# Which score VectorE copies, where v's sums go, and the order of a phase's last four scores

## The chip, the cores and the metric

One core of a Trainium2 chip runs the whole program. The metric is the device time of one execution in microseconds (us). The core has a matrix engine (TensorE: PE in the profile, its weight loads PEld), VectorE (DVE), ScalarE (ACT), GpSimd (POOL) and SyncE (SP), which here issues transfers. Each engine takes its instructions in the order in which they were written, and waits on semaphores for the others. PSUM, the memory that TensorE writes, has eight banks; a tile of 128 x 512 float32 fills one of them.

## What is computed

The kernel mixes a full attention and a token-mixing MLP over the same x (2048 tokens, 512 channels, 32 heads of 16).

```python
g = _sigmoid((x * gate_w).sum(-1, keepdims=True))
# A: attention
q, k, v = split_heads(x @ wqkv)
p = _softmax(einsum("bhqd,bhkd->bhqk", q, k) * Dh ** -0.5)
a = merge_heads(einsum("bhqk,bhkd->bhqd", p, v)) @ wo
# B: token mixing
h = _layernorm(x)
u = _gelu(einsum("bsd,sf->bdf", h, w1) + b1)
b = einsum("bdf,fs->bds", u, w2) + b2, transposed
out = g * a + (1 - g) * b
```

## The kernel before

The first 278 us project v, k and q, and compute the first layer of the MLP. From there to 1232 us runs one long loop, and the change lies in it. The loop has 32 groups (a pair of heads and half of the queries) of 4 phases each, 128 phases in all, numbered p from 0.

**A phase.** A phase computes 16 blocks of scores, numbered n from 0 to 15; a block has 128 keys by 512 queries of one head and fills one PSUM bank. Each block's exp is then multiplied with v, and the products are added up in a PSUM tile `av`. The two heads of a pair lie in the two halves of TensorE's rows, so a score needs only half of the rows. The other half works beside it on a matmul of other work, called dense here (L1049): the MLP's second layer, late parts of the q projection, or the output projection. A phase has either 14 dense matmuls (96 phases, "14-phases") or 12 (32 phases, "12-phases": two in a row at p = 6, 14, 22 and so on to 62, and the last 16, p = 112 to 127). Scores that have no dense partner are written for the other head than the one before them, so that two can run side by side.

**Who evacuates the scores.** ScalarE takes six blocks one by one (`SINGLE`, L1066: exp straight from PSUM) and four as two pairs (`TWO`, L1004: exp over two banks). VectorE copies the other six to SBUF (`EVAC`, L1062), four early in the phase and n = 14 and 15 at its end; one exp over all six (L1075, 128 x 3072) follows. An empty instruction of VectorE (`mark`, L1084) stands behind the copies and gathers waits for that exp. The pairs in `TURNS` are multiplied with v in the same phase, those in `HELD` (the copied ones) in the next.

**Banks.** Seven banks serve the scores, the eighth (`dn`) the dense work. `share` lists the seven for a phase. Scores 0 to 6 take `share[0]` to `share[6]`, scores 7, 8 and 9 take `share[0]`, `[1]`, `[2]` once more, and 10 to 15 take `[3]`, `[4]`, `[5]`, `[6]`, `[0]`, `[1]`. What is left, `share[2]`, becomes `av`. A matmul into a bank waits until the score before it in that bank is read.

**Sums.** At the end of a phase VectorE adds `av` to the group's sums in SBUF (L961). In a group's first phase there are two tiles: `av` closes the group before (from the held pairs), and a second one, in the place of a score pair (`t`), begins the new group. How many adds a tile takes depends on which heads and query halves its pairs hold: all four together are one add of 128 x 512, three of the four are one of 128 x 256 and one of 64 x 256.

**Order around it.** Engines run the loop in the order of the source. `calls` are transfers issued at a phase's beginning, `amid` is work of VectorE that is written ahead of its copy of score 14, and `later` is work of VectorE that is written after the phase's copies, ahead of the adds. The last two blocks of the MLP's gelu (functions `inner`, `tanh`, `outer`, L555 to L565) are spread over `later` of phases 0 to 3. `add_manual_dep(one..., earlier...)` makes the third single exp (n = 4) wait for the second pair's exp of the phase before, on ScalarE itself.

Of the kernel before, what the change touches and what calls it, by code (L numbers as in the profile page):

```python
# [60 lines left out]
def gated_mix(ctx: ExitStack, tc: tile.TileContext, a_x, a_wqkv, a_wo, b_w1, b_b1, b_w2, b_b2, gate_w, out):  # L61
    nc = tc.nc
# [487 lines left out]
        late_u.append((u, at))  # L550
    late_s = o_pool.tile([P, ND, NB], F32, name="big0")

    def inner(i):
        u, s = late_u[i][0], late_s[:, i, :]
        nc.vector.tensor_mul(s, u, u)  # L555
        nc.vector.tensor_scalar(s, s, GELU_A, 1.0, ALU.mult, ALU.add)
        nc.vector.tensor_mul(s, s, u)

    def tanh(i):
# [2 lines left out]
    def outer(i):  # L562
        u, at = late_u[i]
        nc.vector.scalar_tensor_tensor(u, late_s[:, i, :], 1.0, u, ALU.add, ALU.mult)
        split(u_hi[:, at, :], u_lo[:, at, :], u, nc.vector.tensor_copy, nc.vector.tensor_tensor)  # L565

    acc_ctx.close()
# [113 lines left out]
    def on_dve(at, *what):  # L681
        later.setdefault(at, []).append(what)
# [54 lines left out]
    def invert(half, k, pairs, at):  # L737


        n = pairs * 2  # L740
        w = QW // DH
        t = out_pool.tile([P, w], F32, name="inv")[: n * DH]
        nc.sync.dma_start(t, r_d[half][k][:n].rearrange("r (a b) -> (r a) b", b=w))

        def turn():
            nc.vector.tensor_scalar_max(t, t, LEAST_SUM)
            nc.vector.reciprocal(t, t)

        def put_back():
            nc.sync.dma_start(ri_d[half][k][:n].rearrange("r (a b) -> (r a) b", b=w), t)  # L750

        if half and k == ND - 1:
            amid[at + 1] = [turn]
# [91 lines left out]
        return put(steps, at, [len(steps)])  # L845

    for i in range(2):
        on_dve(i, inner, i)
        on_dve(1 + i, tanh, i)
        on_dve(2 + i, outer, i)  # L850
    call(3, load_xt, 2)
    for b in range(ND):
        call(6 + b, nc.sync.dma_start, v_d[b], vb[b][:, :BV])
# [39 lines left out]

    token, mark = (out_pool.tile([1, 1], F32, name=name, bufs=1) for name in ("token", "mark"))

    EVAC = 1, 3, 5, 7, 14, 15
    SINGLE = 0, 2, 4, 6, 8, 9
    TWO = (10, 11), (12, 13)
    TURNS = [(0, 2), (4, 6), (8, 9), *TWO]
    HELD = [(1, 3), (5, 7), (14, 15)]  # L900

    def shares(n):

# [62 lines left out]
    with tc.manual_schedule(engines=engines):  # L966
# [3 lines left out]
        for p in range(LAST + 1):  # L970
# [14 lines left out]
            n_b = len(beside)  # L985
            half = slice(0, HALF) if second else slice(HALF, P)

            alone = NSC - (NSC - n_b) // 2
            head = [second if n < alone else 1 - second for n in range(NSC)]
            in_turn = list(range(n_b)) + [n for pair in zip(range(n_b, alone), range(alone, NSC)) for n in pair]  # L990
            qbs = {}
            for a, b in TURNS + HELD:
                if head[a] == head[b]:
# [21 lines left out]
            for n in in_turn:  # L1015
# [3 lines left out]
                if n < TWO[0][0]:  # L1019
                    if n >= BANKS:  # L1020
                        ones[share[n - BANKS]] = psum.tile([P, NB], F32, name=f"s{share[n - BANKS]}")
                    s = ones[share[n % BANKS]]
                else:
                    if n == TWO[0][0]:
                        pool.__exit__(None, None, None)
                        pool = regions()
                        psum = pool.__enter__()
                        twos = {}
                        for low in range(BANKS):
                            if low == share[2]:  # L1030
# [9 lines left out]
                nc.tensor.matmul(  # L1040
                    s,
# [5 lines left out]
                if n < n_b:  # L1047
# [4 lines left out]
                    if n == n_b - 1:  # L1052
                        fence = nc.gpsimd.memset(token, 0.0)  # L1053
                        tc.add_manual_dep(fence.ins, mm.ins.name, SYNC, reason=REASON)
                if n == HELD[-1][0]:
                    if n_b and second and beside[-1][-1] in between:
                        between[beside[-1][-1]]()
                    for what in amid.get(p, ()):
                        what()
                if n in EVAC:  # L1060
                    pt = evac[:, EVAC.index(n), :]
                    nc.vector.tensor_copy(pt, s)  # L1062
# [1 line left out]
                elif n in SINGLE:  # L1064
                    pt = ptp.tile([P, NB], F32, name="p1", bufs=len(SINGLE))
                    one = nc.scalar.activation(pt, s, AF.Exp, scale=SCALE)  # L1066
# [25 lines left out]
                what(*args)  # L1092
# [186 lines left out]
```

## Time and profile before

| | |
|---|---|
| time, median of 3 runs | 1267.92 us (1267.75 to 1268.17) |
| profiled execution | 1267.55 us, of which the span is 1265.7 |
| PE busy in the span | 1257.1 us (99%) |
| ACT busy | 1071.2 us (85%) |
| DVE busy | 849.1 us (67%) |
| POOL busy | 199.3 us (16%) |
| granted TensorE clock, mean | 0.999 |

The profile is of one execution. A row of the timeline reads: start in us from the span's start, length in us, engine, line of the kernel, operation, what it writes and reads by the program's names, how many were merged, and in brackets the idle time of the engine before it with what ended that. Merged rows overlap, since an instruction's length runs from its start to its result and the next one starts earlier. PE counts as busy while a matmul is in flight, modelled, so a full PE row does not say that TensorE could not go faster.

### The profile page before, as it was taken

How to read it: one execution, taken by the hardware profiler on the slowest of the kernel's cores; microseconds unless marked ns; L12 is line 12 of the kernel's file. 1: busy time of each engine (PE TensorE's matmuls, PEld its weight loads, DVE VectorE, ACT ScalarE, POOL GpSimd, SP SyncE). 2: the span in 40 equal slices, each digit the busy share in tenths (PEclk: the TensorE clock that was granted, in tenths of full speed). 3: DMA queues.
4: the chain of work that ended last, by engine and by line, in shares of the span. 5: the costliest groups of instructions: out<-in, count | busy, mean ns of one | idle time of the engine just before them, and what ended most of it. 6: DMA issues, size and time to landing. Idle time of an engine off the chain costs nothing.

```text
span 1265.7 us, 32791 instructions
## 1 busy us (share of the span) xinstructions
PE 1257.1 (99%) x13342; PEld 838.1 (66%) x13342; DVE 849.1 (67%) x1547; ACT 1071.2 (85%) x1405; POOL 199.3 (16%) x316
## 2 busy tenths in 40 slices
PE   9999999999999999999999999999999999999998
PEld 7888888875666666666666666666666666666666
DVE  5675453178767676767677677776777677678883
ACT  4443343269999999999999999999999999999990
POOL 0220444461010101010110101111111111000000
PEclk9999999999999999999999999999999999999999
DMA  4799443243744544544344433444543443366511
GB/s 134 253 327 342 139 125 104 79 130 96 223 123 100 93 101 85 156 87 97 77 103 96 95 92 85 91 87 80 114 100 76 88 99 60 56 166 176 143 65 70
DMA packets 100555, 152.31 MB, mean 120 GB/s; under 512 B 17109, under 2 KB 56171, under 8 KB 96300
## 3 DMA queue, kind: packets, MB, share of 16 engines
q1 hardware_dynamic: 99820, 149.08, 46.0%
q8 instruction: 107, 1.75, 0.6%
q10 hardware_dynamic: 576, 1.05, 0.2%
q14 instruction: 52, 0.43, 0.1%
HBM read 105.39 MB, written 44.68 MB: 119 GB/s over the span
## 4 chain that ended last, share of the span: by engine, by line
PE 98%; DVE 1%; ACT 1%; DMA 0%; issue 0%; SPq 0%
PE av L939 31%; PE s L1040 22%; PE acc L424 12%; PE acc L75 8%; PE t L1040 8%; PE t L939 5%; PE dn L1049 5%; PE u L1040 4%; PE pa L1131 2%; PE acc L199 1%; PE acc L268 1%; DVE pe L1062 0%; PE pa L1161 0%; ACT p L1066 0%; DMA wv_raw<-in_A_wqkv_dram 0%; ACT pe L1075 0%
## 5 line engine op out<-in xcount | busy, mean ns | idle before, releaser
L1066 ACT ACTIVATE p<-s 128x512 f32<-128x512 f32 x768 | 406.2, 726 | 0.4
L1075 ACT ACTIVATE pe<-pe 128x3072 f32<-128x3072 f32 x129 | 375.6, 2913 | 0.4 <-DVE mark L1084 0.4
L1040 PE MATMUL s<-qs,ks 64*128 64x512 f32 x1280 | 330.1, 400 | 0.8 <-DVE ot L961 0.8
L1062 DVE COPY pe<-s 128x512 f32<-128x512 f32 x512 | 318.0, 684 | 4.6 <-PE s L1040 1.1
L1040 PEld LDWEIGHTS s<-qs,ks 64*128 64x128 f32 x1280 | 225.8, 184 | 91.8 <-issue 51.9
L1004 ACT ACTIVATE p<-t 128x1024 f32<-128x1024 f32 x256 | 268.6, 1188 | 0.0
L939 PE MATMUL av<-p,v 128*32 128x256 f32 x3880 | 227.1, 379 | 0.0
L1062 DVE COPY pe<-u 128x512 f32<-128x512 f32 x256 | 164.9, 686 | 71.4 <-PE u L1040 61.4
L939 PE MATMUL av<-pe,v 128*32 128x256 f32 x3072 | 192.5, 383 | 0.2 <-ACT pe L1075 0.2
L961 DVE TENSOR_TENSOR ot<-av,ot 128x512 f32<-128x512 f32 (+2 forms) x149 | 91.4, 614 | 148.7 <-PE av L939 147.5
L68 POOL TENSOR_TENSOR w_lo<-w_raw,w_hi 128x512 fp32r<-128x512 f32 (+1 forms) x128 | 153.4, 1205 | 196.6 <-ACT w_hi L67 100.0
L1049 PE MATMUL dn<-u_hi,w_hi 64*128 64x512 f32 x448 | 181.3, 405 | 0.0
L939 PEld LDWEIGHTS av<-p,v 128*32 128x32 f32 x3880 | 126.0, 110 | 83.3 <-issue 0.2
L1049 PE MATMUL dn<-u_hi,w_lo 64*128 64x512 f32 x448 | 180.7, 403 | 0.0
L1049 PE MATMUL dn<-u_lo,w_hi 64*128 64x512 f32 x448 | 179.8, 401 | 0.0
L1040 PE MATMUL t<-qs,ks 64*128 64x512 f32 x512 | 154.6, 411 | 0.0
L939 PEld LDWEIGHTS av<-pe,v 128*32 128x32 f32 x3072 | 86.8, 109 | 84.1 <-ACT p L1066 39.0
L1053 POOL MEMSET token<- 1x1 f32 x128 | 11.4, 89 | 749.8 <-PE dn L1049 649.2
L1040 PEld LDWEIGHTS t<-qs,ks 64*128 64x128 f32 x512 | 80.6, 184 | 45.1 <-ACT p L1066 40.6
L67 ACT CAST w_hi<-w_raw 128x512 fp32r<-128x512 f32 (+1 forms) x67 | 38.0, 569 | 82.9 <-PE acc L424 63.1
L424 PE MATMUL acc<-h_hi,w_hi 128*128 128x512 f32 x224 | 87.9, 392 | 0.0
L424 PE MATMUL acc<-h_hi,w_lo 128*128 128x512 f32 x224 | 87.8, 392 | 0.0
(162 smaller groups left out, 1623.8 us busy)
## 6 DMA issues: line engine op xcount, KB each, us to landing
w_raw<-in_B_w_dram SPq DMA_DIRECT2D x96, 256.0 KB
ks<-kp SPq DMA_DIRECT2D x192, 128.0 KB
qs<-qp SPq DMA_DIRECT2D x256, 64.0 KB
kp<-pc SPq DMA_DIRECT2D x16, 512.0 KB
qp<-pc SPq DMA_DIRECT2D x8, 768.0 KB
qp<-row SPq DMA_DIRECT2D x24, 256.0 KB
v<-v SPq DMA_DIRECT2D x4, 1088.0 KB
x<-in_A_x_dram SPq DMA_DIRECT2D x16, 256.0 KB
```

The lines of the kernel that those rows point to most:

```text
L67: copy(hi, src)
L68: return sub(lo, src, hi.bitcast(F32), ALU.subtract)
L75: nc.tensor.matmul(ps, a, b, start=start and n == 0, stop=stop and n == last)
L424: nc.tensor.matmul(p, a, b, start=first and k == 0, stop=last and k == 2)
L939: mm = nc.tensor.matmul(av[32 * j : 32 * (j + 1), i * QC : (i + 1) * QC], vb[b][:, v_at : v_at + 32], pt[:, h * QC : (h + 1) * QC], start= ...
L961: latest["add"] = nc.vector.tensor_tensor(x, y, x, ALU.add)
L1004: pairs_done.append(nc.scalar.activation(pt, twos[low, low + 1], AF.Exp, scale=SCALE))
L1040: nc.tensor.matmul(s, kt[grp][rows_i, c * P : (c + 1) * P], qt[grp][rows_i, qb * NB : (qb + 1) * NB], start=True, stop=True,)
L1049: mm = nc.tensor.matmul(ps, a[half], b[half], start=begin and not second, stop=last and bool(second))
L1062: nc.vector.tensor_copy(pt, s)
L1066: one = nc.scalar.activation(pt, s, AF.Exp, scale=SCALE)
L1075: done = nc.scalar.activation(x, x, AF.Exp, scale=SCALE)
```

## The change

- VectorE copies score 9 in place of score 7, and ScalarE takes 7 singly (`EVAC`, `SINGLE`, `TURNS`, `HELD`).
- `av` takes `share[1]`, where score 8 was, and score 15 takes `share[2]`, where score 9 was. The banks of the phases that follow turn with it (`spare`).
- In 12-phases the last four scores run in the order 12, 13, 15, 14 instead of 12, 14, 13, 15, and the heads of 13 and 15 are exchanged to go with it.
- ScalarE's wait on its own earlier exp moves from the third single (n = 4) to the sixth (n = 8).
- The two late gelus are cut into five steps each. Three of VectorE's steps move ahead of its last two copies (`amid`): the square of the first, the closing product of `inner` for both, `outer`'s product of the second. The rest stays behind the copies, in part a phase later.

```diff
+    def squares(i):
+        nc.vector.tensor_mul(s, u, u)
+    def cubic(i):
+        nc.vector.tensor_scalar(s, s, GELU_A, 1.0, ALU.mult, ALU.add)
     def inner(i):
-        nc.vector.tensor_mul(s, u, u)
-        nc.vector.tensor_scalar(s, s, GELU_A, 1.0, ALU.mult, ALU.add)
         nc.vector.tensor_mul(s, s, u)
...
+    def outer_parts(i):
+        u, at = late_u[i]
         split(u_hi[:, at, :], u_lo[:, at, :], u, nc.vector.tensor_copy, nc.vector.tensor_tensor)
...
     for i in range(2):
-        on_dve(i, inner, i)
         on_dve(1 + i, tanh, i)
-        on_dve(2 + i, outer, i)
+        on_dve(2 + i, outer_parts, i)
+    for p, mid, what, i in (
+        (0, True, squares, 0),
+        (0, False, cubic, 0),
+        (1, True, inner, 0),
+        (1, False, squares, 1),
+        (1, False, cubic, 1),
+        (2, True, inner, 1),
+        (2, False, outer, 0),
+        (3, True, outer, 1),
+    ):
+        if mid:
+            amid.setdefault(p, []).append((what, i))
+        else:
+            later.setdefault(p, []).insert(1 if what is cubic and i else 0, (what, i))
...
-    EVAC = 1, 3, 5, 7, 14, 15
-    SINGLE = 0, 2, 4, 6, 8, 9
+    EVAC = 1, 3, 5, 9, 14, 15
+    SINGLE = 0, 2, 4, 6, 7, 8
...
-            alone = NSC - (NSC - n_b) // 2
-            head = [second if n < alone else 1 - second for n in range(NSC)]
-            in_turn = list(range(n_b)) + [n for pair in zip(range(n_b, alone), range(alone, NSC)) for n in pair]
+            head = [second if n < n_b else (second + NSC - 1 - n) % 2 for n in range(NSC)]
+            if n_b == NSC - 2:
+                head[-2:] = second, 1 - second
+            else:
+                head[-4:] = second, 1 - second, 1 - second, second
+            in_turn = list(range(n_b)) + ([14, 15] if n_b == NSC - 2 else [12, 13, 15, 14])
...
-                            if low == share[2]:
+                            if low == share[1]:
                                 av = psum.tile([P, NB], F32, name="av")
-                            elif low in share[:2]:
+                            elif low in (share[0], share[2]):
                                 twos[low] = psum.tile([P, NB], F32, name=f"u{low}")
...
-                    s = twos[share[(n - BANKS) % BANKS]]
+                    s = twos[share[2 if n == NSC - 1 else (n - BANKS) % BANKS]]
...
-                if n == HELD[-1][0]:
+                if n == in_turn[-2]:
...
-                    if n == SINGLE[2] and p:
+                    if n == SINGLE[-1] and p:
                         tc.add_manual_dep(one.ins, earlier.ins.name, SYNC, reason=EARLY)
...
-            spare = share[2]
+            spare = share[1]
```

**TensorE at the end of a 12-phase** (p = 6). In the names `t5`, `t1`, `u0`, `u3` the digit is the bank; `t` holds a pair of scores, `u` a single one that VectorE will copy. Before:

```order
L1049 MATMUL dn_3371<-big0_2984,row_3119 128x512
L1040 MATMUL t0_3426<-qs1_2583,ks1_2582 128x512
L1040 MATMUL u3_3428<-qs1_2583,ks1_2582 128x512
L1040 MATMUL t0_3426<-qs1_2583,ks1_2582 128x512
L1040 MATMUL u4_3429<-qs1_2583,ks1_2582 128x512
L939 MATMUL av_3427<-pe_3251,v0_111 32x256 x12
```

Now:

```order
L1074 MATMUL dn_3371<-big0_2984,row_3119 128x512
L1065 MATMUL t1_3427<-qs1_2583,ks1_2582 128x512 x2
L1065 MATMUL u0_3426<-qs1_2583,ks1_2582 128x512
L1065 MATMUL u3_3428<-qs1_2583,ks1_2582 128x512
L961 MATMUL av_3429<-pe_3251,v0_111 32x256 x12
```

The pair's two scores now stand next to each other, and so do the two that VectorE copies; before, each of the pair's stood beside one of the copied.

**VectorE from a 12-phase's last copies to the next phase's first** (p = 116, the first phase of a group). `ot` are a group's sums, `o_sum` and `e` belong to the output projection's inputs. Before:

```order
L1062 COPY pe_17035<-u4_17092 128x512
L1084 MEMSET mark_2618 1x1
L1092 TENSOR_TENSOR o_sum_16772<-e2_16771,o_sum_16772 128x512
L1092 CAST e2_16771<-o_sum_16772 128x512
L1092 TENSOR_TENSOR e2_16771<-o_sum_16772,e2_16771 128x512
L961 TENSOR_TENSOR ot_16501<-av_17090,ot_16501 128x512
L961 TENSOR_TENSOR ot_17015<-t5_17093,ot_17015 128x256
L1062 COPY pe_17163<-s2_17169 128x512
```

Now:

```order
L1087 COPY pe_17044<-u3_17100 128x512
L1109 MEMSET mark_2618 1x1
L1117 TENSOR_TENSOR o_sum_16781<-e2_16780,o_sum_16781 128x512
L1117 CAST e2_16780<-o_sum_16781 128x512
L1117 TENSOR_TENSOR e2_16780<-o_sum_16781,e2_16780 128x512
L983 TENSOR_TENSOR ot_16509<-av_17101,ot_16509 128x256
L983 TENSOR_TENSOR ot_16509<-av_17101,ot_16509 64x256
L983 TENSOR_TENSOR ot_17024<-t5_17102,ot_17024 128x256
L983 TENSOR_TENSOR ot_17024<-t5_17102,ot_17024 64x256
L1087 COPY pe_17174<-s2_17180 128x512
```

Both tiles now hold three of the four combinations of head and query half, and each takes one add more.

**VectorE in phases 0 and 3**, around the late gelu: from the fourth copy to the next phase's first. Before, phase 0:

```order
L1062 COPY pe_2636<-s3_2672 128x512
L1062 COPY pe_2636<-u3_2692 128x512
L1062 COPY pe_2636<-u4_2693 128x512
L555 TENSOR_TENSOR big0_2588<-row_2584 128x512
L556 TENSOR_SCALAR big0_2588<-big0_2588 128x512
L557 TENSOR_TENSOR big0_2588<-big0_2588,row_2584 128x512
L961 TENSOR_TENSOR ot_2621<-av_2691,ot_2621 128x256
L1062 COPY pe_2746<-s4_2754 128x512
```

Now, phase 0:

```order
L1087 COPY pe_2636<-s2_2682 128x512
L555 TENSOR_TENSOR big0_2588<-row_2584 128x512
L1087 COPY pe_2636<-u3_2692 128x512
L1087 COPY pe_2636<-u2_2691 128x512
L559 TENSOR_SCALAR big0_2588<-big0_2588 128x512
L983 TENSOR_TENSOR ot_2621<-av_2693,ot_2621 128x256
L1087 COPY pe_2745<-s2_2751 128x512
```

The square (L555) has moved ahead of the last two copies and the closing product (L557) out of the phase. Phase 3 before, where `w_hi` is a weight of the second layer and `u_hi`, `u_lo` are the gelu's two parts:

```order
L1062 COPY pe_2988<-u4_3045 128x512
L1084 MEMSET mark_2618 1x1
L67 CAST w_hi_3066<-w_raw_2632 128x512
L564 SCALAR_TENSOR_TENSOR row_2586<-big0_2588,row_2586 128x512
L67 CAST u_hi_1293<-row_2586 128x512
L68 TENSOR_TENSOR u_lo_1294<-row_2586,u_hi_1293 128x512
L961 TENSOR_TENSOR ot_2621<-av_3042,ot_2621 128x512
```

Phase 3 now:

```order
L570 SCALAR_TENSOR_TENSOR row_2586<-big0_2588,row_2586 128x512
L1087 COPY pe_2988<-u1_3043 128x512
L1087 COPY pe_2988<-u0_3042 128x512
L1109 MEMSET mark_2618 1x1
L67 CAST w_hi_3067<-w_raw_2632 128x512
L67 CAST u_hi_1293<-row_2586 128x512
L68 TENSOR_TENSOR u_lo_1294<-row_2586,u_hi_1293 128x512
L983 TENSOR_TENSOR ot_2621<-av_3044,ot_2621 128x512
```

The product of `outer` (L564, now L570) has moved ahead of the copies. SyncE's transfers and GpSimd's instructions stand in the order they had.

More of the change, by code (lines that the diff above doesn't have):

```diff
@@ L551, in gated_mix @@
     late_s = o_pool.tile([P, ND, NB], F32, name="big0")
+    def squares(i):
+        u, s = late_u[i][0], late_s[:, i, :]
+        nc.vector.tensor_mul(s, u, u)
+    def cubic(i):
+        s = late_s[:, i, :]
+        nc.vector.tensor_scalar(s, s, GELU_A, 1.0, ALU.mult, ALU.add)
     def inner(i):
         u, s = late_u[i][0], late_s[:, i, :]
-        nc.vector.tensor_mul(s, u, u)
-        nc.vector.tensor_scalar(s, s, GELU_A, 1.0, ALU.mult, ALU.add)
         nc.vector.tensor_mul(s, s, u)
@@ L752, in invert @@
         if half and k == ND - 1:
-            amid[at + 1] = [turn]
+            amid[at + 1] = [(turn,)]
             on_dve(at + 1, put_back)
@@ L894, in gated_mix @@
     token, mark = (out_pool.tile([1, 1], F32, name=name, bufs=1) for name in ("token", "mark"))
-    EVAC = 1, 3, 5, 7, 14, 15
-    SINGLE = 0, 2, 4, 6, 8, 9
+    EVAC = 1, 3, 5, 9, 14, 15
+    SINGLE = 0, 2, 4, 6, 7, 8
     TWO = (10, 11), (12, 13)
-    TURNS = [(0, 2), (4, 6), (8, 9), *TWO]
-    HELD = [(1, 3), (5, 7), (14, 15)]
+    TURNS = [(0, 2), (4, 6), (7, 8), *TWO]
+    HELD = [(1, 3), (5, 9), (14, 15)]
     def shares(n):
@@ L1054, in gated_mix @@
                         tc.add_manual_dep(fence.ins, mm.ins.name, SYNC, reason=REASON)
-                if n == HELD[-1][0]:
+                if n == in_turn[-2]:
                     if n_b and second and beside[-1][-1] in between:
                         between[beside[-1][-1]]()
-                    for what in amid.get(p, ()):
-                        what()
+                    for what, *args in amid.get(p, ()):
+                        what(*args)
                 if n in EVAC:
```

## The prediction

> **What bounds the kernel now.** I read the page first, then busy times by stretches of the loop, then the timeline of one phase of each kind.
>
> ```profile
> span 1265.7 us, 32791 instructions
> PE 98%; DVE 1%; ACT 1%; DMA 0%; issue 0%; SPq 0%
> L1066 ACT ACTIVATE p<-s 128x512 f32<-128x512 f32 x768 | 406.2, 726 | 0.4
> ```
>
> The chain gives PE 98%, but PE's ends are modelled. The stretches say more. Columns are stretch, us, then busy us (count) of PE, PEld, DVE, ACT, POOL, PE clock, DMA share, GB/s; the stretches are phases 0 to 5, 6 to 63, 64 to 111, 112 to 127:
>
> ```profile
> 278.00:324.40 46.40, 45.57 (x544) 27.44 (x546) 38.14 (x66) 45.87 (x58) 10.53 (x14) 1.00 0.47 118
> 324.40:755.40 431.00, 430.67 (x5422) 268.72 (x5420) 302.17 (x566) 430.98 (x524) 44.68 (x101) 1.00 0.47 108
> 755.40:1111.40 356.00, 356.00 (x4514) 222.00 (x4512) 253.30 (x479) 356.00 (x434) 45.60 (x90) 1.00 0.41 86
> 1111.40:1232.40 121.00, 120.33 (x1478) 74.73 (x1474) 98.86 (x175) 120.74 (x146) 3.98 (x20) 1.00 0.54 141
> ```
>
> ACT is full as well, and the third stretch has only 14-phases: 356.00/48 = 7.417 us each. Is that PE's pace or ScalarE's? In a series of 14-phases:
>
> ```profile
> 574.32 2.86 ACT L1075 ACTIVATE pe<-pe 128x3072 f32<-128x3072 f32 x1
> 581.87 2.81 ACT L1075 ACTIVATE pe<-pe 128x3072 f32<-128x3072 f32 x1
> 589.20 2.90 ACT L1075 ACTIVATE pe<-pe 128x3072 f32<-128x3072 f32 x1
> 596.54 2.97 ACT L1075 ACTIVATE pe<-pe 128x3072 f32<-128x3072 f32 x1
> 603.94 2.99 ACT L1075 ACTIVATE pe<-pe 128x3072 f32<-128x3072 f32 x1
> 611.35 3.00 ACT L1075 ACTIVATE pe<-pe 128x3072 f32<-128x3072 f32 x1
> ```
>
> The phase before the second row is a 12-phase (7.55). Then the exps start 7.33, 7.34, 7.40 and 7.41 apart, but end 7.42, 7.41, 7.42 and 7.42 apart (584.68, 592.10, 599.51, 606.93, 614.35), while their length grows from 2.81 to 3.00. Work enters ScalarE faster than it leaves, until a backlog of 0.19 is full. So 7.417 is ScalarE's own pace, and TensorE could turn in 7.33. What is lost is what ScalarE stands empty beyond 7.417 a phase:
>
> - phases 0 to 5: 46.40 - 6 x 7.417 = 1.90, of which two tanh on ScalarE are about 1.04: 0.86 lost;
> - 6 to 63: 431.0 - 58 x 7.417 = 0.81, in eight pairs of 12-phases;
> - 112 to 127: 121.0 - 16 x 7.417 = 2.33, or 7.56 a phase.
>
> **The order in 12-phases.** First p = 116, VectorE, TensorE and ScalarE from the fourth copy to the first matmul with v:
>
> ```profile
> 1141.84 2.48 DVE L1062 COPY pe<-s 128x512 f32<-128x512 f32 x4
> 1144.38 0.18 PEld L1040 LDWEIGHTS u<-qs,ks 64*128 64x128 f32 x1 [0.35 <-DVE pe L1062]
> 1144.71 0.39 PE L1040 MATMUL u<-qs,ks 64*128 64x512 f32 x1
> 1141.61 3.05 ACT L1066 ACTIVATE p<-s 128x512 f32<-128x512 f32 x6
> 1145.04 0.16 PEld L939 LDWEIGHTS av<-pe,v 128*32 128x32 f32 x8 [0.36 <-ACT p L1066]
> 1146.33 2.82 ACT L1075 ACTIVATE pe<-pe 128x3072 f32<-128x3072 f32 x1
> 1148.63 0.18 PEld L1040 LDWEIGHTS s<-qs,ks 64*128 64x128 f32 x1 [0.41 <-issue]
> ```
>
> The copies end at 1144.32; 0.06 later score 14 loads, beside 13; score 15 follows alone 0.33 later (1144.71), v another 0.33 later, and 3.59 after that the next phase. From load to v are 0.66. The row names ACT as the releaser of v, but the sixth single's exp ended at 1144.66; the last in time was score 15. A 14-phase does 14 and 15 side by side:
>
> ```profile
> 608.27 0.39 PE L1040 MATMUL s<-qs,ks 64*128 64x512 f32 x1
> 608.67 0.68 DVE L1062 COPY pe<-s 128x512 f32<-128x512 f32 x1
> 609.40 0.21 PEld L1040 LDWEIGHTS u<-qs,ks 64*128 64x128 f32 x2 [0.17 <-DVE pe L1062]
> 606.63 3.24 ACT L1066 ACTIVATE p<-s 128x512 f32<-128x512 f32 x6
> 609.92 0.16 PEld L939 LDWEIGHTS av<-pe,v 128*32 128x32 f32 x8 [0.31 <-ACT p L1066]
> ```
>
> There v could load 0.10 + 0.33 = 0.43 after 609.40, at 609.83; it waits for the sixth single's exp (609.87) until 609.92. With both last scores side by side a 12-phase has 0.43 in place of 0.66, and its turn falls from 7.56 to 7.33. That is under 7.417, so ScalarE becomes the bound there too, and I price a 12-phase at 7.417. Middle: -0.8 (all of the 0.81). End: at most -2.33, less 0.2, because the last exp counts to its end and a full backlog makes it 3.00 long, where it is 2.82 there now: -2.1.
>
> **The tenth score's copy and the banks.** The tenth score (608.27) ends at 608.66, the fourth copy starts at 608.67 today. Copies begin 0.03 to 0.04 after their score (609.94 after 609.90 for the fifth), so the fourth moves by 0.02 to 0.03; from 609.83 to 609.92 the 14-phase has 0.09 of room. Score 15 now waits for this copy, score 14 for the fifth single's exp, about 0.49 before the sixth's end; v still waits for the sixth. Price in 96 14-phases: from 0 to what a later copy costs (rivals); I take 0, because start and end of the copy are set by rows. With a 12-phase turn of 7.36 the statement above holds.
>
> **ScalarE's moved wait.** It waits for the second pair's exp of the phase before; ScalarE runs the large exp (2.8) and five singles between that and the sixth single, so it is long done. ScalarE stood 0.4 us ahead of all 768 singles (the page's row). Between 0 and -0.4: I take 0. Behind a late wait the pairs and the large exp would queue.
>
> **More adds in the last sixteen phases.** VectorE in p = 116 to 117:
>
> ```profile
> 1147.31 0.69 DVE L1092 TENSOR_TENSOR e<-o_sum,e 128x512 fp32r<-128x512 f32 x1
> 1147.92 0.68 DVE L961 TENSOR_TENSOR ot<-av,ot 128x512 f32<-128x512 f32 x1
> 1148.82 0.42 DVE L961 TENSOR_TENSOR ot<-t,ot 128x256 f32<-128x256 f32 x1 [0.22 <-issue]
> 1149.40 0.69 DVE L1062 COPY pe<-s 128x512 f32<-128x512 f32 x1 [0.15 <-PE s L1040]
> L961 DVE TENSOR_TENSOR ot<-av,ot 64x256 f32<-64x256 f32 x20 | 8.6, 428 | 0.6
> ```
>
> Now `av` takes 0.42 + 0.43 in place of 0.68, and `t` one 64x256 more, 0.43. VectorE then ends near 1149.24 + 0.43 + 0.1 = 1149.8, where the copy began at 1149.40: up to 0.4 late after p = 116, 120, 124, perhaps 0.25 after 112, where less stands ahead. The next phase's fourth copy, its last scores and v are late with it. Bounds: 0 if other slack covers it, 4 x 0.43 = 1.7 at most. Of 1.45 I take 0.8, since the gained 0.2 of each such phase and the room of 0.09 cover the rest. End: -2.1 + 0.8 = -1.3.
>
> **The gelu's steps.** Phases 0 to 1 and 3 to 4 before:
>
> ```profile
> 282.75 0.68 DVE L555 TENSOR_TENSOR big<-row 128x512 f32<-128x512 f32 x1
> 283.46 1.91 DVE L556 TENSOR_SCALAR big<-big 128x512 f32<-128x512 f32 x1
> 285.40 0.69 DVE L557 TENSOR_TENSOR big<-big,row 128x512 f32<-128x512 f32 x1
> 285.60 3.10 ACT L1066 ACTIVATE p<-s 128x512 f32<-128x512 f32 x6
> 286.34 1.28 DVE L1062 COPY pe<-s 128x512 f32<-128x512 f32 x2
> 306.56 0.68 DVE L564 SCALAR_TENSOR_TENSOR row<-big,row 128x512 f32<-128x512 f32 x1
> 306.73 1.66 POOL L68 TENSOR_TENSOR w_lo<-w_raw,w_hi 128x512 fp32r<-128x512 f32 x1 [1.74 <-DVE w_hi L67]
> 307.28 1.40 DVE L67 CAST u_hi<-row 128x512 fp32r<-128x512 f32 x1
> 309.17 3.19 ACT L1066 ACTIVATE p<-s 128x512 f32<-128x512 f32 x6
> 309.92 1.28 DVE L1062 COPY pe<-s 128x512 f32<-128x512 f32 x2
> ```
>
> The first copy normally starts 0.24 after ScalarE's first single (1141.84, 606.87 against 606.63). In p = 1 it is 0.74 behind (286.34 to 285.60), in p = 4 0.75 (309.92 to 309.17): 0.50 late each. Less 0.09 of room, 0.41 each, which is the 0.86. Phase 0 loses two products of 0.69 behind its copies, more than 0.50, and the square now runs where VectorE stood 0.59 idle ahead of score 14's copy: that part is won. In phase 3 the product (0.68) goes too, but the cast then begins near 306.6, and GpSimd's w_lo at 306.73 took 1.66; beside it the cast took 1.40. Bounds -0.4 (cast still 1.4 and later) to -0.8. I take -0.7, because the cast would now begin ahead of w_lo. The Trainium skill ("SBUF — State Buffer", section "SBUF: two separate sides") says that a shared port pair of VectorE and GpSimd is locked by whichever instruction starts first, for its whole length; by that the cast goes first and the term is -0.8.
>
> **Sum.** -0.8 - 1.3 - 0.7 = -2.8 on a profiled execution of 1267.55 (span 1265.7 and 1.85 around it): 1264.75. The runs' median, 1267.92, is 0.37 above that execution, so 1265.1. I call 0.2% (2.54 us: under 1265.38) about what a measurement of this kernel can tell from no change. SyncE and GpSimd keep their order and cost nothing.
>
> **Rivals.**
>
> - *The end and the start give less*: every added add late by 0.43 (1.7 in place of 0.8) and the cast still slow (-0.4). -0.8 - 0.4 - 0.4 = -1.6: 1266.3, unchanged.
> - *ScalarE is the floor of 12-phases already*: only the start is gained, 1267.2, unchanged. Against it speak the sixth single of p = 116, done 0.38 before v loads, and the exp shrunk to 2.81 after a 12-phase. The Trainium skill ("ScalarE: Activation LUTs", "What ACT_TABLE_LOAD costs") gives 0.833 ns an element and some 93 ns between overlapping instructions; my estimate from it is 9 x 0.093 + 8192 x 0.000833 = 7.66 a phase, above 7.56. The 7.417 of 48 phases contradicts it.
> - *The fourth copy comes late in 14-phases* (slower): if the tenth score or the copy's start is late by L, 96 phases lose L - 0.09 each. At L = 0.12 the gain is gone, at 0.146 it is over 0.2% slower, at 0.2 it costs 10.6: 1275.7. For it speaks that the 14-phase's load of the last scores already waits for VectorE (0.17, row 609.40), so that nothing but 0.09 covers it; against it, that the tenth score is done 0.01 before the copy starts today.
> - *7.417 isn't ScalarE's own pace* but comes from v waiting for the sixth single, which is an earlier score now: 14-phases too go to 7.36, another 96 x 0.057 = 5.5: 1259.6. Against it: the backlog in the rows above.
>
> **Chances.** Forecast 0.62, of which 0.42 below 1265.38; less gain 0.13; floor 0.06; late copy 0.14; faster 14-phases 0.05. Faster 0.42 + 0.05 = 0.47; slower 0.14; same 0.20 + 0.13 + 0.06 = 0.39. The range leaves out the late copy and the fast 14-phases, 0.19. Its ends: all three terms at their best, -0.8 - 2.1 - 0.8 = -3.7, and 1 us more for what moves between the stretches, 1263.2; and no gain with the runs' spread of 0.25, 1268.2.
>
> **What the changed kernel's profile would show.** The last sixteen phases take 119.7 in place of 121.0, the large exps there are 3.00 long, and the load ahead of v in a 12-phase comes 0.43 after that of the last scores. Phases 64 to 111 stay at 356.0. Phases 0 to 5 take 45.7, with first copies 0.24 behind the first single in p = 1 and 4. I am wrong if the 48 phases differ from 356.0 by over 1 us, with large exps shrunk to 2.8 and the last scores' load behind a copy that ends late; or if phases after 112, 116, 120, 124 turn in 7.8.

## The result, and the profile after

| | before | changed |
|---|---|---|
| median of 12 runs | 1268.14 us (1267.75 to 1268.32) | 1266.72 us (1266.33 to 1267.14) |
| profiled execution | 1267.55, span 1265.7 | 1266.69, span 1264.9 |
| ratio to before | | 0.9989 (95% interval 0.998 to 0.9998) |

The change gains 1.4 us where 2.8 were forecast; the time lies in the range and within the 0.2% that were called no change. (Of the runs below, one of the eleven executions of "before, 15 more" took 3151 us; it is left out of that run's median and ratio.) The profiled execution of before was 0.6 under the median of its runs, so the two spans differ by 0.8 only.

The page of the changed kernel, its span, the chain by engine and the row of the large exp, with that row of the kernel before last:

```profile
span 1264.9 us, 32830 instructions
PE 95%; DVE 2%; ACT 2%; DMA 0%; issue 0%; SPq 0%; DVEq 0%; ACTq 0%
L1100 ACT ACTIVATE pe<-pe 128x3072 f32<-128x3072 f32 x129 | 380.6, 2952 | 0.6 <-DVE pe L1087 0.6
L1075 ACT ACTIVATE pe<-pe 128x3072 f32<-128x3072 f32 x129 | 375.6, 2913 | 0.4 <-DVE mark L1084 0.4
```

The chain now runs over VectorE and ScalarE in places, and the large exp waits 0.6 us for VectorE's copies where it waited 0.4 for the mark. Since phases end earlier now, the stretches are cut anew so that each holds the same phases as in the table before (0 to 5, 6 to 63, 64 to 111, 112 to 127):

```profile
278.00:323.73 45.73, 45.17 (x544) 27.07 (x546) 37.50 (x66) 45.63 (x58) 10.19 (x14) 1.00 0.48 123
323.73:754.06 430.33, 430.25 (x5425) 263.64 (x5422) 306.17 (x574) 430.33 (x524) 44.66 (x101) 1.00 0.47 108
754.06:1109.97 355.91, 355.91 (x4514) 219.98 (x4511) 255.50 (x480) 355.91 (x434) 45.60 (x90) 1.00 0.41 86
1109.97:1230.26 120.29, 119.20 (x1478) 72.46 (x1474) 101.43 (x182) 119.65 (x146) 3.97 (x20) 1.00 0.57 142
```

Start 46.40 to 45.73 (-0.67), middle 431.00 to 430.33 (-0.67), 356.00 to 355.91 (-0.09), last sixteen phases 121.00 to 120.29 (-0.71): ScalarE's last exp ends 2.1 us earlier. The span is only 0.8 shorter, so 1.3 are lost behind the loop. There the engines meet at a last barrier. The page of line L1300 of the changed kernel lists its instructions by engine with first and last start, and SyncE's waits name whom it stood for:

```profile
L1300 ACTq EVENT_SEMAPHORE  x2: 17/17/17, 1263.3 to 1264.9; - x2
L1300 DVEq EVENT_SEMAPHORE  x2: 21/21/21, 1264.6 to 1264.9; - x2
SPq L1300 <- DVEq L1300: 1.2, 1, 1.2
```

ScalarE takes the barrier's release at 1263.3, VectorE only at 1264.6. In the kernel before the same two rows read:

```profile
L1275 ACTq EVENT_SEMAPHORE  x2: 17/17/17, 1265.1 to 1265.7; - x2
L1275 DVEq EVENT_SEMAPHORE  x2: 21/21/21, 1265.1 to 1265.7; - x2
```

So there are three questions: which part gains what, why the last sixteen phases give about half of what was forecast, and what holds VectorE up at the end.

### The profile page after: what moved, and what is told of

Its sections match the earlier page's. It is cut to its first block, busy times and chain, and to the rows that moved or that the text cites. A ratio compares the mean times of both kernels' runs of the same rounds, so it can differ in the third digit from the quotient of the medians.

```text
span 1264.9 us, 32830 instructions
## 1 busy us (share of the span) xinstructions
PE 1255.3 (99%) x13342; PEld 828.8 (66%) x13342; DVE 857.4 (68%) x1562; ACT 1069.2 (85%) x1405; POOL 198.9 (16%) x316
## 3 DMA queue, kind: packets, MB, share of 16 engines
q8 instruction: 107, 1.75, 0.6%
## 4 chain that ended last, share of the span: by engine, by line
PE 95%; DVE 2%; ACT 2%; DMA 0%; issue 0%; SPq 0%; DVEq 0%; ACTq 0%
PE av L961 30%; PE s L1065 20%; PE acc L424 12%; PE acc L75 8%; PE t L1065 8%; PE t L961 5%; PE dn L1074 4%; PE u L1065 3%; PE pa L1156 2%; DVE pe L1087 2%; ACT pe L1100 1%; ACT p L1091 1%; PE acc L199 1%; PE acc L268 1%; ACT p L1029 0%; DVE ot L983 0%
## 5 line engine op out<-in xcount | busy, mean ns | idle before, releaser
L1091 ACT ACTIVATE p<-s 128x512 f32<-128x512 f32 x768 | 412.2, 786 | 0.1
L1100 ACT ACTIVATE pe<-pe 128x3072 f32<-128x3072 f32 x129 | 380.6, 2952 | 0.6 <-DVE pe L1087 0.6
L1087 DVE COPY pe<-s 128x512 f32<-128x512 f32 x512 | 323.9, 686 | 5.5 <-PE s L1065 1.7
L1029 ACT ACTIVATE p<-t 128x1024 f32<-128x1024 f32 x256 | 277.6, 1259 | 0.0
L1065 PE MATMUL t<-qs,ks 64*128 64x512 f32 x512 | 142.2, 412 | 0.0
L1065 PEld LDWEIGHTS t<-qs,ks 64*128 64x128 f32 x512 | 73.1, 184 | 50.9 <-ACT p L1091 48.8
```

Source lines behind the costliest of these rows:

```text
L1029: pairs_done.append(nc.scalar.activation(pt, twos[low, low + 1], AF.Exp, scale=SCALE))
L1065: nc.tensor.matmul(s, kt[grp][rows_i, c * P : (c + 1) * P], qt[grp][rows_i, qb * NB : (qb + 1) * NB], start=True, stop=True,)
L1100: done = nc.scalar.activation(x, x, AF.Exp, scale=SCALE)
```

## The experiments

All times are medians, compared with the kernel before on the same chip (1267.9 to 1268.23). "Start" is everything up to the end of phase 5. Where phases are compared, it is by the ends of their large exps. "Behind the loop" is the time from ScalarE's last exp to the end of the span (33.3 before, 34.7 changed).

| run | time | ratio (95% interval) | start | 6 to 67 | 112 to 127 | behind the loop |
|---|---|---|---|---|---|---|
| changed kernel | 1266.72 | 0.9989 (0.998 to 0.9998) | -0.66 | -0.82 | -0.70 | +1.34 |
| gelu alone | 1266.94 | 0.9994 (0.9985 to 1.0003) | -0.47 | -0.04 | -0.09 | +0.08 |
| order alone | 1267.39 | 0.9996 (0.9987 to 1.0005) | +0.12 | -0.75 | -1.14 | +1.69 |
| banks, tenth score, wait | 1265.57 | 0.9981 (0.9972 to 0.999) | +0.44 | -0.82 | -1.88 | +0.24 |
| wait alone | 1268.14 | 0.9999 (0.999 to 1.0009) | -0.09 | +0.11 | -0.08 | +0.02 |
| changed, old order | 1264.46 | 0.9971 (0.996 to 0.9982) | -0.66 | -0.82 | -1.89 | +0.36 |
| changed, 14 ahead of 15 | 1266.67 | 0.9987 (0.9978 to 0.9996) | -0.25 | -0.84 | -1.15 | +1.57 |
| changed, work spread | 1269.16 | 1.0008 (0.9999 to 1.0017) | -0.82 | -0.80 | +1.57 | +1.77 |
| changed, 30 more | 1265.77 | 0.9984 (0.9975 to 0.9993) | -0.87 | -0.83 | -0.63 | +0.18 |
| before, 15 more | 1269.81 | 1.0014 (1.0005 to 1.0024) | -0.01 | +0.04 | +0.04 | +1.32 |

The last four columns are the profiled execution's difference to that of before, one execution each. The middle is taken to phase 67, four phases behind the last pair of 12-phases; in the changed kernel 6 to 63 give -0.67 of it. The intervals of gelu alone, order alone, wait alone and work spread include 1, so these four times can't be told from before's, and what they show stands in the stretches. The start scatters by some 0.2 from run to run, and that comes from ahead of the loop: ScalarE's exp of phase 0, which no part of the change touches, ends between 285.5 and 286.3.

### The gelu's steps alone

```diff
-        on_dve(i, inner, i)
-        on_dve(2 + i, outer, i)
+        on_dve(2 + i, outer_parts, i)
+    ... (squares, cubic, inner and outer put as in the changed kernel)
```

> The kernel before with the gelu's steps as in the changed kernel, nothing else. In the changed kernel's trace ScalarE finishes phase 5 earlier by 0.66 us, won in phases 1 (0.40) and 4 (0.29). Theory: those come from the gelu's steps alone, so phase 5 ends 0.6 to 0.7 earlier here too and nothing else changes: 0.7 us under before. Rival (the start was won by the tenth score's copy or the banks): phase 5 ends as before and the time is before's.

Phases 1 and 4 are shorter by 0.40 and 0.30, as in the changed kernel (0.40, 0.29), and the 0.2 between that and the table's 0.47 stand in phase 0. The start's gain is the gelu's. (Four of VectorE's steps stand ahead of its last two copies, not three: both closing products, the first square and the second product of `outer`.)

### The order alone

```diff
-            head = [second if n < alone else 1 - second for n in range(NSC)]
-            in_turn = list(range(n_b)) + [n for pair in zip(range(n_b, alone), range(alone, NSC)) for n in pair]
...
+                head[-4:] = second, 1 - second, 1 - second, second
+            in_turn = list(range(n_b)) + ([14, 15] if n_b == NSC - 2 else [12, 13, 15, 14])
```

> The kernel before with the heads and the order of the last four scores of 12-phases as in the changed kernel, nothing else. Theory: phases 6 to 67 give 0.8 us and the last sixteen give 0.7 (12 phases shorter by 0.14 each, and the phases after 112, 116, 120, 124 longer by 0.06 to 0.32 for the added adds), so ScalarE's last exp ends about 1.5 earlier than before. Rival 1: the order needs the new banks, so 12-phases stay at 7.55 and the time is before's. On the end of the program: VectorE's program has 15 instructions more here, as in the changed kernel, whose VectorE came 1.2 us late to the last barrier. If that goes by the number of its instructions, it is late here too and the time falls by 0.3 to 0.9 only; if it was chance or belongs to the other parts, the time falls by 1.5.

p = 116 of this run, VectorE's first copies and TensorE's loads of the last scores and of v:

```profile
1140.66 2.48 DVE L1065 COPY pe<-s 128x512 f32<-128x512 f32 x4
1143.24 0.19 PEld L1043 LDWEIGHTS u<-qs,ks 64*128 64x128 f32 x2 [0.30 <-ACT p L1069]
1143.73 1.02 PEld L939 LDWEIGHTS av<-pe,v 128*32 128x32 f32 x24 [0.30 <-ACT p L1069]
```

The two last scores load together, and v 0.59 after the copies' end (1143.14) where it was 0.72: the step of the prediction holds. With the old banks score 15, which now comes first of the two, takes the bank of score 8, and that is read by ScalarE; so it is ScalarE's exp that releases the loads, and not the copy. The last sixteen phases gave 1.14 where I expected 0.7: phases 117, 121 and 125 take 7.45, 7.52 and 7.49, and 118, 122 and 126 about 7.60. VectorE is late behind the loop, as in the changed kernel.

### The tenth score's copy, the banks and the wait

```diff
+    EVAC = 1, 3, 5, 9, 14, 15
+    SINGLE = 0, 2, 4, 6, 7, 8
...
+                            if low == share[1]:
                                 av = psum.tile([P, NB], F32, name="av")
...
+                    s = twos[share[2 if n == NSC - 1 else (n - BANKS) % BANKS]]
...
+                    if n == SINGLE[-1] and p:
```

> The kernel before with VectorE's copy of the tenth score, the banks of av and score 15 and ScalarE's moved wait, nothing else. Theory: nothing on the path: 14-phases 7.42, 12-phases 7.55 to 7.58, time within 0.3 us of before. Rival (the fourth copy comes late): 14-phases above 7.42, the time up by 96 times the difference. Rival (ScalarE's wait held something back): the time falls by up to 0.4.

My theory fell: these parts, priced at nothing, give as much in the middle as the order does, and more at the end, 2.3 us in all. p = 116 and the last sixteen phases:

```profile
1141.13 2.55 DVE L1062 COPY pe<-s 128x512 f32<-128x512 f32 x4
1143.53 0.18 PEld L1040 LDWEIGHTS u<-qs,ks 64*128 64x128 f32 x1 [0.22 <-ACT p L1066]
1143.73 0.18 PEld L1040 LDWEIGHTS u<-qs,ks 64*128 64x128 f32 x1
1144.19 1.02 PEld L939 LDWEIGHTS av<-pe,v 128*32 128x32 f32 x24 [0.28 <-ACT p L1066]
1111.07:1230.18 119.11, 118.85 (x1478) 75.44 (x1474) 99.64 (x175) 119.09 (x146) 3.95 (x20) 1.00 0.56 144
```

Score 14 now sits where score 7 was, which ScalarE reads, so it loads at 1143.53, ahead of the copies' end (1143.68). Only score 15 waits for the fourth copy; it loads 0.05 after it and v 0.46 later, 0.51 behind the copies' end in place of 0.72. That is enough for ScalarE to be the bound: v waits for its exp (0.28). So the order and these parts both remove the same loss, and either alone is enough. By the rows it is the exchange of the copies of 7 and 9 that frees score 14, while the move of the banks puts score 15 behind a copy; no run takes the two apart.

Phase 4 is 0.42 longer here. It is the cast of phase 3 that the prediction spoke of, VectorE and GpSimd:

```profile
307.26 1.87 DVE L67 CAST u_hi<-row 128x512 fp32r<-128x512 f32 x1
306.71 1.67 POOL L68 TENSOR_TENSOR w_lo<-w_raw,w_hi 128x512 fp32r<-128x512 f32 x1 [1.76 <-DVE w_hi L67]
308.33 0.52 POOL L975 MEMSET ot<- 128x512 f32 x1
```

The cast takes 1.87 where it took 1.40, and ends at 309.13, 0.28 after the end of GpSimd's following memset. In the changed kernel the gelu's steps have moved, and phase 4 is shorter.

### The wait alone

```diff
-                    if n == SINGLE[2] and p:
+                    if n == SINGLE[-1] and p:
```

> The kernel before with ScalarE's wait on its own exp moved from the third to the sixth single, nothing else. Theory: it costs and gives nothing, every phase as before, time within 0.3 us. Rival: the 2.3 us of the run with banks, tenth score and this wait come from the wait; then 12-phases fall from 7.55 to 7.42 here.

1268.14 against 1268.23, and the 12-phases at the end take 7.52 to 7.57 as before: the wait gives nothing, as priced.

### The changed kernel with the order of before

```diff
-                head[-4:] = second, 1 - second, 1 - second, second
-            in_turn = list(range(n_b)) + ([14, 15] if n_b == NSC - 2 else [12, 13, 15, 14])
+            alone = NSC - (NSC - n_b) // 2
+            head = [second if n < alone else 1 - second for n in range(NSC)]
+            in_turn = list(range(n_b)) + [n for pair in zip(range(n_b, alone), range(alone, NSC)) for n in pair]
```

> The changed kernel with the heads and the order of the last four scores of 12-phases as before (12, 14, 13, 15), everything else as changed. The banks and the tenth score's copy alone took all of the 0.14 off each 12-phase, middle (0.82) and end (1.88). New theory: either the new order or the new banks suffices for that, the order adds only its twenty adds and the late end; so here the start gains 0.66 to 0.87, the middle 0.8, the end 1.9, VectorE isn't late at the end: 3.4 under before, near 1264.5. Rival: the two parts need each other once the gelu's steps have moved, and it is no faster than the banks alone (2.3 under before).

1264.46, 3.5 under before and faster than both kernels. (The order's added adds are 15, the difference of the 1562 and 1547 instructions of VectorE on the two pages; the twenty of the expectation were miscounted.) Its first and last stretch (0 to 5, 112 to 127):

```profile
278.00:323.74 45.74, 45.16 (x546) 27.24 (x546) 37.56 (x66) 45.66 (x58) 10.20 (x14) 1.00 0.47 122
1109.98:1229.08 119.10, 118.84 (x1478) 75.38 (x1474) 99.57 (x175) 119.08 (x146) 3.96 (x20) 1.00 0.56 143
```

The last sixteen take 119.10, 7.44 a phase, where the changed kernel takes 120.29. So the order costs 1.2 there and 1.0 (1.34 - 0.36) behind the loop.

### What the order costs in the last sixteen phases

Two things could make the phases after 112, 116, 120 and 124 long: the added adds, or the order of scores 14 and 15. p = 120 to 121 in the changed kernel, ScalarE's first single, VectorE, the loads and the large exp:

```profile
1177.24 3.25 ACT L1091 ACTIVATE p<-s 128x512 f32<-128x512 f32 x6
1177.17 0.87 DVE L983 TENSOR_TENSOR ot<-t,ot 128x256 f32<-128x256 f32 x2
1178.06 2.49 DVE L1087 COPY pe<-s 128x512 f32<-128x512 f32 x4
1180.60 0.19 PEld L1065 LDWEIGHTS u<-qs,ks 64*128 64x128 f32 x2 [0.32 <-DVE pe L1087]
1181.13 1.29 DVE L1087 COPY pe<-u 128x512 f32<-128x512 f32 x2 [0.58 <-PE u L1065]
1182.51 2.77 ACT L1100 ACTIVATE pe<-pe 128x3072 f32<-128x3072 f32 x1 [0.20 <-DVE pe L1087]
```

The first copy starts 0.82 behind the first single, 0.58 later than the usual 0.24; score 15, which waits for the fourth copy, comes first and holds 14 too; VectorE idles 0.58, and the large exp waits for its last copies. In the next run 14 comes first:

```diff
-                head[-4:] = second, 1 - second, 1 - second, second
+                head[-4:] = second, 1 - second, second, 1 - second
-            in_turn = ... [12, 13, 15, 14]
+            in_turn = ... [12, 13, 14, 15]
```

> The changed kernel with 12-phases' last scores in the order 12, 13, 14, 15 and their heads exchanged to go with it. The added adds and VectorE's 1971 instructions stay as in the changed kernel; but score 14, which doesn't wait for the tenth score's copy, now stands ahead of 15, which does. Theory: phases 117, 121 and 125 are long (7.75, 7.87, 7.83) because the late fourth copy holds both last scores, so VectorE's last two copies and with them the large exp come 0.3 later than in the run with the order alone; here they fall by 0.2 to 0.3 each, to the 7.45 to 7.55 of that run, and the time by 0.6 to 0.9 under the changed kernel. Rival: the adds alone make them long, and they stay above 7.7.

```profile
1177.37 3.18 ACT L1091 ACTIVATE p<-s 128x512 f32<-128x512 f32 x6
1180.22 0.19 PEld L1065 LDWEIGHTS u<-qs,ks 64*128 64x128 f32 x1
1180.65 0.18 PEld L1065 LDWEIGHTS u<-qs,ks 64*128 64x128 f32 x1 [0.24 <-DVE pe L1087]
1180.88 1.29 DVE L1087 COPY pe<-u 128x512 f32<-128x512 f32 x2 [0.28 <-PE u L1065]
1182.26 2.77 ACT L1100 ACTIVATE pe<-pe 128x3072 f32<-128x3072 f32 x1
```

Score 14 loads 0.43 ahead of 15, VectorE idles 0.28 in place of 0.58, and the exp starts 4.89 behind the first single, where it was 5.27. Phases 117, 121, 125 fall from 7.75, 7.87, 7.83 to 7.41, 7.42, 7.42, but part of it comes back in 118, 122 and 126 (7.63, 7.69, 7.70, from 7.45, 7.41, 7.41). The last sixteen go from -0.70 to -1.15 against before. So of the 1.19 that the order costs there (-1.89 to -0.70), 0.45 is the order of 14 and 15, and 0.74 is left, nearly all of it in 118, 122 and 126. The run with the order alone falls short of the run with the banks alone, which has no added adds, by 0.74 too (-1.14 to -1.88). I lay it to the adds, but no run takes them away and keeps the order. The time does not show the 0.45, where I expected 0.6 to 0.9: 1266.67 is 1.56 under its before, and the changed kernel was 1.42 under. In the profiled execution the start came 0.4 later and VectorE 0.2 later behind the loop.

The other try was to clear the place of the adds (VectorE's work on the output projection's inputs goes to other phases):

```diff
-        call(p0 + k, fetch_right, k, p0 + k + 2, p0 + k + 2, p0 + k + 2)
+        call(p0 + k, fetch_right, k, *((p0 + 3, p0 + 5, p0 + 5) if k == 2 else (p0 + k + 2,) * 3))
...
-    call(p0 + 6, fetch_o, 1, p0 + 8, p0 + 8, p0 + 10)
+    call(p0 + 6, fetch_o, 1, p0 + 9, p0 + 9, p0 + 10)
...
-    call(p0 + 9, fetch_o, 2, p0 + 11, p0 + 12, p0 + 12)
+    call(p0 + 9, fetch_o, 2, p0 + 11, p0 + 13, p0 + 13)
```

> The changed kernel with VectorE's work on the output projection's inputs moved out of phases 116, 120 and 124 (it follows in 115 and 117, 121, 125), so that the added adds stand alone behind those phases' copies. Theory (the first copies of 117, 121, 125 are late because this work and the adds stand ahead of them): these phases fall from 7.75, 7.87, 7.83 to about 7.42, and the last sixteen gain about 1.0 more; the late end stays. Rival (they are long because the two last scores wait for the tenth score's copy together, whatever stands ahead): they stay above 7.6.

It took 2.4 us more than the changed kernel. Phases 117, 121 and 125 fell only to 7.66, 7.62 and 7.57, and others became late, 116, 118, 122 and 126 (7.85, 8.52, 8.14, 8.09). 118 is the worst, since 117 had work of its own:

```profile
1154.24 0.69 DVE L1117 TENSOR_TENSOR o_sum<-e,o_sum 128x512 f32<-128x512 f32 x1
1156.03 0.68 DVE L983 TENSOR_TENSOR ot<-av,ot 128x512 f32<-128x512 f32 x1
1156.63 2.47 DVE L1087 COPY pe<-s 128x512 f32<-128x512 f32 x4
```

The first copy stands right behind a full queue of VectorE, as in 121 of the changed kernel. It does not tell how much of the 0.74 is the adds' own length and how much the work ahead of them.

### VectorE's late end

The page of the changed kernel counts 1562 instructions of VectorE, that of before 1547. (The two expectations below say 1971 and 1956 by a count that no page shows; the difference of 15 is the same.) Two runs change that number with memsets of one element, one in each of phases 20 to 49 or 20 to 34.

```diff
+    for p in range(20, 50):                  # after: 30; before: range(20, 35)
+        on_dve(p, nc.vector.memset, pad, 0.0)
```

> The changed kernel with one more tiny instruction of VectorE (a memset of one element, 0.06 us) in each of phases 20 to 49, behind its copies. Theory (VectorE waits at the end for its instructions, and where that falls goes by their number): the 1.2 us between the last barrier's release and VectorE's answer vanish, and the time falls by about 1.2 below the changed kernel, 2.6 below before. Rival 1 (chance, or a late transfer): the gap stays or the time does not differ from the changed kernel's. Rival 2 (the added instructions hold up the copies): 14-phases from 20 to 49 longer than 7.42, at most 30 x 0.06 = 1.8 us in all.

> The kernel before with one more tiny instruction of VectorE in each of phases 20 to 34, so that VectorE's program has as many instructions as the changed kernel's (1971 in place of 1956). Theory (the place of VectorE's last instructions in its program makes it late at the end): the span from ScalarE's last exp to the end is 34.7 to 35.0 in place of 33.3, and the time is about 1.3 above before. Rival (the late end belongs to the added adds or to chance): 33.3 to 33.6, the time as before.

SyncE's waits at the end, first of the changed kernel with 30 more, then of before with 15 more:

```profile
SPq L1302 <- PEq L1302: 0.6, 2, 0.5
```

```profile
SPq L1277 <- DVEq L1277: 1.4, 1, 1.4
SPq L1277 <- PEq L1277: 0.4, 2, 0.3
```

With 30 more the wait for VectorE is gone, 1.16 of the 1.34 behind the loop with it, and the time is 2.1 under before where the changed kernel was 1.4 under. With 15 more it is there in the kernel before, 1.4 long, and the time rises by 1.8, while each stretch of the loop stays within 0.04. Of the 13 profiles here the six with 1562 instructions (changed, order, 14 first, spread, 15 more, and the short exp below) have 34.5 to 35.1 behind the loop, and the seven with 1547, 1592 or 1658 have 33.3 to 33.8. So the number of VectorE's instructions decides, and with it the place of its last ones in its program. That it is the loading of instructions is argued, not shown: the wait is on VectorE's own sequencer (DVEq), behind its last branch (L1223, 1259.0), and in the changed kernel's 1.3 us between ScalarE's answer and VectorE's the trace has no work of VectorE and only two transfers, packets of 8 KB of an instruction queue (q14). In each of the six such a packet also starts 2.10 to 2.13 before the end of the span, 1.75 to 1.78 ahead of VectorE's last-but-one answer, and in the seven others none starts between 2.4 and 1.6 before the end. That fits a load that VectorE waits for, but the trace doesn't tell which engine a packet is for.

### ScalarE's own pace, and the room of the fourth copy

Two runs test terms that the forecast left at nothing in 14-phases. The first makes ScalarE shorter: it leaves 24 columns of each copied block without exp.

```diff
-            for x in ([evac] if p < LAST else ...
+            for x in ([evac[:, :, : NB - 24]] if p < LAST else ...
```

> The changed kernel, where the large exp leaves out the last 24 columns of each of its six blocks (144 of 3072 elements a row, raw scores stay there), to make ScalarE 0.12 us a phase shorter. Theory (7.417 is ScalarE's own pace, TensorE could turn in 7.33 to 7.36): 14-phases fall to 7.33 to 7.36, the time by about 110 x 0.07 = 8 us. Rival (7.417 is TensorE's or the pace of the wait of v for the sixth single): 14-phases stay at 7.42. If TensorE had more room than I read, they fall to 7.30.

Time 1261.09, 5.6 under the changed kernel. ScalarE's large exps, and phases 64 to 111:

```profile
586.53 2.72 ACT L1100 ACTIVATE pe<-pe 128x2928 f32<-128x2928 f32 x1
593.92 2.72 ACT L1100 ACTIVATE pe<-pe 128x2928 f32<-128x2928 f32 x1
601.32 2.72 ACT L1100 ACTIVATE pe<-pe 128x2928 f32<-128x2928 f32 x1
751.42:1105.02 353.60, 353.60 (x4512) 234.65 (x4510) 255.43 (x480) 353.56 (x433) 45.55 (x90) 1.00 0.41 86
```

353.60/48 = 7.367 a phase: it fell by 0.05, and not by the 0.13 taken from ScalarE (my estimate: 144 of the 3072 elements of an exp of 2.81), and the exps stay at 2.72. So 7.417 is ScalarE's own pace, and the turn of TensorE with the copies in it is 7.37, 0.03 above what I read from exps that started 7.33 apart. The second run delays the fourth copy:

```diff
                 if n in EVAC:
+                    if n == EVAC[3] and n_b == NSC - 2:
+                        nc.vector.memset(probe, 0.0)
```

> The changed kernel with a memset of 128x256 on VectorE ahead of the fourth copy in each of the 96 14-phases, which delays that copy by d (some 0.2 to 0.4 us; the trace gives it). Theory (the prediction's rival: only some 0.09 us of room): each 14-phase grows by d less 0.05 to 0.09, with the load of the last scores behind the copy and no backlog at ScalarE, so 10 to 33 us in all. Rival (the copy isn't on TensorE's path and has more room): 14-phases stay at 7.42.

```profile
598.25 2.55 DVE L1087 COPY pe<-s 128x512 f32<-128x512 f32 x4
601.60 1.89 DVE L1090 COPY pe<-s 128x512 f32<-128x512 f32 x3
603.49 0.27 DVE L1088 MEMSET probe<- 128x256 f32 x1
603.68 0.63 DVE L1090 COPY pe<-s 128x512 f32<-128x512 f32 x1
604.36 0.18 PEld L1066 LDWEIGHTS u<-qs,ks 64*128 64x128 f32 x1 [0.21 <-DVE pe L1090]
606.04 2.85 ACT L1103 ACTIVATE pe<-pe 128x3072 f32<-128x3072 f32 x1
758.96:1120.68 361.72, 361.72 (x4512) 233.61 (x4510) 263.62 (x528) 360.92 (x433) 45.52 (x90) 1.00 0.41 84
```

The first row is the changed kernel's: there the fourth copy ends 2.55 behind the first one's start. With the memset it ends at 604.31, 2.71 behind (601.60), so 0.16 later; the median of phases 66 to 109 is 0.18. Score 15 loads 0.05 after it. The 48 phases take 361.72, 7.536 each, 0.12 more. The time is 1276.87 (1.0067, 1.0049 to 1.0086), 10.2 above the changed kernel. So the room of the fourth copy is what the 0.16 to 0.18 have over the 0.12, some 0.05.

## Why the prediction was right, and where it was off

Direction and range were right, the size was half. That the time stayed in the range is in part luck: 1.34 us went at a place for which the sum has no term, and the range held because it reached up to no gain. By its steps:

- *ScalarE's pace bounds 14-phases, and they stay*: right. 356.23 (by ends of exps) became 356.13.
- *Middle, -0.8*: measured -0.82 (-0.67 up to phase 63). The mechanism that I named works: in p = 116 of the changed kernel v loads 0.43 after the last scores (1142.99 and 1142.56), and the order alone gives -0.75. But the exchanged copies with the banks, priced at zero, do the same alone (-0.82), and with them in place the order adds nothing (changed, old order: -0.82). I had seen that score 14 would wait for the fifth single and not for the copy, and did not carry it into the 12-phases.
- *Start, -0.7*: measured -0.66, 0.40 and 0.29 in the two phases named. What I took from the Trainium skill ("SBUF — State Buffer", "SBUF: two separate sides") for the cast is borne out. In the changed kernel it starts 0.17 ahead of GpSimd's w_lo and takes 0.42 in place of 1.40; where it started behind w_lo, it ended only after it (0.29 after, at 308.68):

```profile
306.19 0.42 DVE L67 CAST u_hi<-row 128x512 fp32r<-128x512 f32 x1
306.36 1.40 POOL L68 TENSOR_TENSOR w_lo<-w_raw,w_hi 128x512 fp32r<-128x512 f32 x1 [1.77 <-DVE w_hi L67]
308.72 2.76 ACT L1091 ACTIVATE p<-s 128x512 f32<-128x512 f32 x5
308.95 2.53 DVE L1087 COPY pe<-s 128x512 f32<-128x512 f32 x4
```

  The first copy of p = 4 is 0.23 behind the first single, as forecast. In p = 1 more was cleared than the sum had: the cubic took 0.82 in place of 1.91, and the first copy came at 284.60, ahead of the first single (285.58), which waited for ScalarE's own large exp.
- *End, -2.1 + 0.8 = -1.3*: this term was mis-sized; it measured -0.70. The gain without the order's costs is 1.89, so 2.1 was near, though it comes without the order too. Of the order's cost 0.74, which I lay to the adds, is near 0.8. What I missed is 0.45: where VectorE is late, score 15, standing ahead of 14, hands that on to both last copies and the large exp. I looked at how late the first copy comes (0.4 said, 0.58 measured in 121) and not at what stands behind the fourth. A sign of being wrong that I had named came here: phases 117, 121 and 125 turn in 7.75, 7.87 and 7.83 (113 in 7.48), and the large exps of the last sixteen are 2.77 to 2.90 long, not 3.00.
- *The tenth score's copy, 0*: right in 14-phases. The room was some 0.05 rather than 0.09; by the rival's rule a copy that ends 0.16 to 0.18 late would cost 0.07 to 0.09 a phase, and it cost 0.12.
- *ScalarE's wait, 0*: right.
- *The end of the program*: the sum had no term for it. It gave back 1.34 in the profile, the largest miss. Of 2.8 forecast, 0.6 went to the last sixteen phases and 1.3 here; what is left, some 0.8, is the difference of the spans, and the medians' 1.4 differ from it by the 0.6 by which before's profiled execution was fast.

The time came nearest to the rival of less gain (1266.3, chance 0.13), but only in small part by its mechanism: the order cost 1.19 at the end, between the 0.8 of the forecast and the rival's 1.7, but the start gave nearly all that was forecast, and the larger loss lay where no rival looked.

## What to carry to other kernels

When two parts of a change aim at the same wait, price each alone and then the second on top of the first: here the exchanged copies with the banks were enough, the order added only its costs, and the changed kernel without it (1264.46) is faster than both. A late engine is judged by what waits behind its last instruction in that phase, so among several scores put the one that waits least first. And compare the time behind the loop as well: a few added instructions can move an engine's end by over 1 us with no work in it.

## What the hardware showed that was not expected

VectorE answers a barrier at the program's end 1.0 to 1.4 us late by SyncE's waits when the page counts 1562 instructions of it, and not at 1547, 1592 or 1658. The Trainium skill ("Runtime: NRT & Kernel Launch", section "Instruction fetch mechanics") says that instructions come in blocks, that crossing a block's border is mostly hidden, and that a taken branch breaks the loading ahead. The runs fit a border that comes behind VectorE's last branch in the six late programs, whose crossing then is not hidden; they don't show that the packets seen there are VectorE's.

A cast on VectorE took 0.42, 1.40 or 1.87 us for the same 128 x 512, by whether it started ahead of GpSimd's instruction, beside it, or beside it and the one that followed. In the two slow cases it ended 0.29 and 0.28 after GpSimd's.
